# Values' products of the first four steps in other PSUM rings, sink rows on one queue, the next four steps' values two slots later

## The chip, the cores and the metric

The kernel runs on one core of a Trainium2 chip. The metric is the device time of one execution in microseconds (us). The engines are called PE (TensorE, matrix products), PEld (its weight loads), DVE (VectorE), ACT (ScalarE), POOL (GpSimd) and SP (SyncE, which issues most DMAs). Every engine works through its own list of instructions in order.

## The reference, cut to what matters

Attention with a sliding window of 128 keys and 4 sink keys over q, k, v of shape (4, 8, 768, 64), and then a feed-forward block over the 3072 rows of its result:

```python
keep = is_sink | in_window                 # rel in [0, 128) or key < 4
a = softmax(where(keep, scale * q @ k.T, -1e9))
x = (a @ v).transpose(0, 2, 1, 3).reshape(B * S, H * D)      # 3072 x 512
h = x @ w_in                               # 512 -> 2048
g = h * erf(softplus(h))
out = g @ w_out                            # 2048 -> 512
```

## The kernel before, in words

The 3072 rows are 12 groups of 256 tokens. Attention for a group is 4 steps, one per pair of heads, so step s belongs to group s // 4, and there are 48 steps. A step runs through these stages, each a small function in the code: `prep` transposes k and q on PE into a PSUM tile `tqk` and ACT copies it to `kq` (L299, L302, L305); `core` makes the scores `ps` on PE (L350), DVE adds the mask and takes the row maximum (L363, L368) and ACT the exponentials (L372); `norm` divides by the sums (L379 to L391, for steps 2 to 7 the division runs on ACT at L385); `ptrans` transposes the probabilities into PSUM tiles `tp` and `ts` (L403, L404), ACT copies them to `pa` and `pz` (L410 to L416) and POOL cuts the window's triangles out of them with four selects (L421); `av` multiplies them with the values on PE into a PSUM tile `av` (L452), from the values themselves and from `vz`, a tile that holds the sinks' 16 rows and half blocks of values; `xfin` copies the result to x on ACT (L465 for group 0; L470, and L471 on DVE, for the others).

PSUM has eight banks, dealt out as rings: `ps_o` two (tag o, the output sums), `ps_h` two (tag h, the hidden tiles), `ps_s` one tile of two banks (the scores), `ps_t` two (tag t: tqk, tp, ts and av take turns). A tile that takes a slot of a ring waits until the slot's last reader is done.

The feed-forward block goes by f: 16 blocks of 128 hidden units. A hidden tile h_m covers two f (L639 for group 0 in plain 32-bit products, L643 for the others in three products of split operands, called xh, xl and wt). ACT makes six activations of it (L656 to L661), DVE multiplies three of them together (L665, result gf, for the first two groups), and PE multiplies the result with w_out into the sums o (L685 for the first two groups, L688 to L690 for the others). The weights are 32 blocks (0 to 15 of w_in, 16 to 31 of w_out). They arrive as 64-bit floats (ws), and DVE turns each block into 32-bit with three passes (L541, L546, L549, result wf). All 32 are converted while groups 0 and 1 are under way.

The order of the work is set by a plan in slots (one slot per f): `plan[a]` lists what is emitted in slot a, `pos(s)` gives the slot of a step's scores (s for the first four steps, 3s - 6 for the next four), and a table of priorities goes with it. A scheduler then merges all engines' work by these priorities, so that a change of one slot or ring shuffles many neighbours. `norm` stands at pos + 1, `ptrans` at pos + 2, `av` at pos + 3, `xfin` at pos + 4. From step 8 on, av runs right before the scores of a later step.

In the first group the loads are issued in a list `head`. The sinks' rows for vz are eight small DMAs (`early_sinks(z, i, h)`): four for z = 1 on SP's queue, four for z = 0 on ACT's queue (L246), behind its first copy of keys (`mark["k"]`).

Of the kernel before, what the change touches and what calls it, by code (L numbers as in the profile page):

```python
# [9 lines left out]
F32 = mybir.dt.float32  # L10
# [9 lines left out]
P = 128  # L20
SW = 16
# [18 lines left out]
NE, AL = 4, 2  # L40
# [12 lines left out]
def kernel(  # L53
# [11 lines left out]
    nc = tc.nc  # L65
    B, H, S, D = q.shape
    NT, DM = out.shape
# [4 lines left out]
    GT = 256  # L72
# [58 lines left out]
    def fast_path():  # L131
        with ExitStack() as st:
# [5 lines left out]
            ps_o = st.enter_context(tc.tile_pool(name="ps_o", bufs=2, space=PSUM))  # L138
            ps_h = st.enter_context(tc.tile_pool(name="ps_h", bufs=2, space=PSUM))
            ps_s = st.enter_context(tc.tile_pool(name="ps_s", bufs=1, space=PSUM))  # L140
            ps_t = st.enter_context(tc.tile_pool(name="ps_t", bufs=2, space=PSUM))
# [25 lines left out]
            def set_rest():  # L167

                follow(mark["t", 0], nc.vector.tensor_tensor(mask[:, :P], kw[:, :128], kw[:, 128:256], op=ALU.max))
                set_mask(mask)  # L170
                set_flags(lambda ins: follow(mark["t", 0], ins))
# [10 lines left out]
            kq = pers.tile([P, NPAIR, 5, KB], F32, name="kq")  # L182
# [10 lines left out]
            mark = {}  # L193
# [49 lines left out]
            def early_sinks(z, i, h):  # L243

                r0 = HP * (1 - z) + 2 * SW * i + SW * h
                ins = (nc.sync if z else nc.scalar).dma_start(  # L246
                    vz[r0 : r0 + SW, z, i].rearrange("p (c h) d -> p c h d", h=2)[:, :, h],
                    v[0, :, :SW].rearrange("(c h) s d -> s c h d", h=2)[:, :, h],
                )
                if not z:  # L250
                    follow(mark["k"], ins)

            def early_dup(z, n):

# [3 lines left out]
            def next_dup():  # L258

                nc.sync.dma_start(vz[lo, 0], early[1, "v"][lo])  # L260
                for n in range(2):
                    nc.sync.dma_start(vz[hi, 1, n], early[n, "v"][hi, 1 - n])

            def dup(s):
# [3 lines left out]
                nc.sync.dma_start(vz[lo, 0, :, cs], t[lo, 1:])  # L268
                x = t[hi, 1:2].broadcast_to([HP, 2, 2, D]) if g % GPB == 0 else t[hi, :2]
                nc.sync.dma_start(vz[hi, 1, :, cs], x)  # L270

            def zero_sinks(s):

                for i in range(2):
                    for h in range(2):
                        early_sinks(0, i, h)

            def kcopy(s):

# [3 lines left out]
            def follow(prev, ins):  # L283

                if prev is not None:
                    tc.add_manual_dep(
                        ins.ins, prev.ins.name,
                        mybir.DependencyInfo(mybir.DependencyClass.NoSync, mybir.DependencyReason.DATA), reason="order",
                    )
                return ins  # L290

            def prep(s):

                g, c = divmod(s, NPAIR)
                d = stp[s]
                tp = ps_t.tile([P, 4, P], F32, tag="t", name=f"tqk_{s}")
                for j, t in enumerate((d["k"], d["q"])):
                    for i in range(2):
                        nc.tensor.transpose(  # L299
                            out=tp[:, 2 * j + i, :], in_=t[:, i].rearrange("p h d -> p (h d)"), identity=ident  # L300
                        )
                nc.scalar.copy(kq[:, c, 1:, :P], tp)  # L302
                if g % GPB == 0:
                    x = tp[:, 0, :SW].rearrange("p (o t) -> p o t", o=1)
                    mark.setdefault("k", nc.scalar.copy(kq[:, c, :3, P:], x.broadcast_to([P, 3, SW])))  # L305

            def core(s):

                prev = None
                late = s - AL >= 2 * NPAIR  # L310
                if late:
                    prev = av(s - AL)
                if s < NSTEP:
                    score(s, prev)
# [115 lines left out]
            def av(s):  # L430

                g, c = divmod(s, NPAIR)
                d = stp[s]
                gb = g % GPB
                a = d["av"] = ps_t.tile([P, GT], F32, tag="t", name=f"av_{s}")
                vt, pz = d["v"], d["pz"]
                pa = d["pa"].rearrange("p h i t -> p h (i t)")
                ops = []
                for j, (t0, t1) in enumerate(((0, HP), (HP, 3 * HP), (3 * HP, GT))):
                    if j > 0 or gb > 0:  # L440
                        x = vt[j] if isinstance(vt, list) else vt[:, j]
                        ops.append((x, pa[:, :, t0:t1], t0))
                for i in range(2):
                    for z, hf in enumerate((lo, hi)):
                        ops.append((vz[:, z, i, 2 * c : 2 * c + 2], pz[:, :, i, hf], P * i + HP * z))
                prev = mark.get(("p", s + 1)) if 0 < s < NE - 1 else None
                for m, (x, y, t0) in enumerate(ops):
                    for h in range(2):
                        o = a[64 * h : 64 * h + 64, t0 : t0 + y.shape[-1]]
                        prev = follow(  # L450
                            prev,
                            nc.tensor.matmul(  # L452
                                o, x[:, h, :], y[:, h, :], start=(m == 0), stop=(m == len(ops) - 1), skip_group_check=True
                            ),
                        )
                return prev
# [21 lines left out]
            def pos(s):  # L478

                return s if s < NE else 3 * s - 6 if s < 2 * NPAIR else 4 * s - 11  # L480

            plan = {}
            for s in range(NSTEP + AL):
                if s < NSTEP:
                    for what, fn, a in (
                        ("prep", prep, max(4, s - 1) if NE <= s < 2 * NPAIR else pos(s) - 3), ("norm", norm, pos(s) + 1), ("ptrans", ptrans, pos(s) + 2),
                        ("load", load, pos(s) - 4),
                    ):
                        if what == "load":
                            if s < 2 * NPAIR:  # L490
                                continue
                            plan.setdefault(a, []).append(("load", load_v, s))
                        plan.setdefault(max(a, 0 if what == "prep" else -1), []).append((what, fn, s))
                    if s >= 2 * NPAIR:
                        plan.setdefault(pos(s) - 2, []).append(("dup", dup, s))
                    if s // NPAIR % GPB < GPB - 1:
                        plan.setdefault(pos(s) + (2 if s < NE else 1), []).append(("kcopy", kcopy, s))
                plan.setdefault(pos(s), []).append(("core", core, s))
                if s < 2 * NPAIR:
                    plan.setdefault(pos(s) + 3, []).append(("av", av, s))  # L500
                    plan.setdefault(pos(s) + 4, []).append(("xfin", xfin, s))
                elif s - AL >= 2 * NPAIR:
                    plan.setdefault(pos(s) + 1, []).append(("xfin", xfin, s - AL))
            STAGES = ("xfin", "norm", "ptrans", "av", "kcopy", "prep", "core", "dup", "load")
# [66 lines left out]
            head = [(early_load, 0, "k", two[0]), (early_load, 0, "q", two[0], nc.scalar)]  # L571
            head += [(early_load, 0, nm, two[1]) for nm in "kq"] + [(wload, order[0])]
            head += [(early_load, 0, nm, four) for nm in "kq"] + [(early_load, 0, "v", slice(0, H))]
            head += [(early_dup, z, n) for z in range(2) for n in range(2)]
            head += [(early_sinks, 1, i, h) for i in range(2) for h in range(2)]
            head += [(wload, n) for n in order[1:4]]
            head += [(wload, order[4])] + [(early_load, 1, nm, slice(0, H)) for nm in "kq"]
            head += [(wload, n) for n in order[5:8]] + [(early_load, 1, "v", slice(0, H))] + [(wload, n) for n in order[8:W0]]
            for x, (fn, *args) in enumerate(head):
                with at(-1 + 4 * x / PW, "load"):  # L580
                    fn(*args)
            plan.setdefault(2 * NE, []).append(("dup", lambda s: next_dup(), NE))
            plan.setdefault(0, []).append(("load", zero_sinks, 0))
            plan.setdefault(2, []).append(("prep", lambda s: set_rest(), NSTEP))
            for m in range(-LEAD, NG * NF + LAG + 2):
                a = m + LEAD
                live = 0 <= m < NG * NF
                if live:
                    g, f = divmod(m, NF)
# [107 lines left out]
    def general_path():  # L697

        NT_S = S // P
        with ExitStack() as st:  # L700
# [71 lines left out]
            with tc.tile_pool(name="g_one1", bufs=1) as one, tc.tile_pool(name="g_work1", bufs=2) as work:  # L772
# [3 lines left out]
                with tc.For_i(0, B, 1) as b:  # L776
                    for gb in range(GPB):
# [25 lines left out]
                        for i in range(2):  # L803
# [3 lines left out]
                            )  # L807

    fast_path()
    ok = nc.values_load(flagi[0:1, 0:1], min_val=0, max_val=1)  # L810
    with tc.If(ok == 0):  # L811
# [31 lines left out]
```

## Time and profile before

| | |
|---|---|
| three runs, us | 748.79, 748.98 (median), 750.62 |
| the profiled execution: its time / its span, us | 748.7 / 746.5 |
| busy share PE, DVE, ACT, POOL | 96%, 65%, 74%, 28% |
| chain that ended last | PE, in the output products of the last group |

The shares are averages over the whole span; the change touches only the first 100 us, and from there on the instruction lists of both kernels soon run alike.

### The profile page before, as it was taken

To read this page: it belongs to the slowest core of one execution; us is meant where nothing else is said; L and a number is where in the kernel's file an instruction comes from. 1 tells how busy PE (TensorE), PEld (TensorE's weight loads), DVE (VectorE), ACT (ScalarE), POOL (GpSimd) and SP (SyncE) were. 2 spreads that over 40 slices of the span, in tenths; PEclk is the share of its full clock that TensorE was granted. 3 is DMA by queue.
4 is the path that set the end of the run, shared out by engine and by line. 5 is a ranking of instruction groups with operands and counts; after the bars stand their busy time and mean duration, and the time that the engine had idled before them with its cause. 6 is when DMAs were issued, how large, how long until landed. Compare 5 with 4: busy or idle time off the path is not lost. (4 is left out here: it accounts for less than half of the span.)

```text
span 746.5 us, 16409 instructions
## 1 busy us (share of the span) xinstructions
PE 717.5 (96%) x5808; PEld 598.3 (80%) x5808; DVE 487.1 (65%) x1367; ACT 553.7 (74%) x1317; POOL 207.0 (28%) x296
## 2 busy tenths in 40 slices
PE   5769999999899999999999999999999999999997
PEld 3557666766788888888888888888888898889885
DVE  6999976755676666665665665666566576475252
ACT  4687666984996975985985976886886786777572
POOL 1322412012242232233233234224223223333221
PEclk9689999999999999999999999999999999999999
DMA  7999311111312211311311321221221222200000
GB/s 148 301 318 363 88 29 43 35 34 43 87 34 57 79 37 43 83 37 42 79 41 46 80 47 34 74 50 40 69 54 41 76 48 45 61 18 2 29 1 33
DMA packets 115113, 53.60 MB, mean 72 GB/s; under 512 B 93840, under 2 KB 107664, under 8 KB 115024
## 3 DMA queue, kind: packets, MB, share of 16 engines
q1 hardware_dynamic: 114144, 52.33, 26.5%
q8 instruction: 49, 0.80, 0.4%
q14 instruction: 40, 0.33, 0.2%
q10 hardware_dynamic: 880, 0.13, 0.1%
HBM read 38.54 MB, written 6.29 MB: 60 GB/s over the span
## 5 line engine op out<-in xcount | busy, mean ns | idle before, releaser
L643 PE MATMUL h<-xh,wt 128*128 128x256 f32 x1408 | 277.8, 286 | 0.7 <-DVE u L665 0.7
L643 PEld LDWEIGHTS h<-xh,wt 128*128 128x128 f32 x1408 | 224.2, 188 | 7.5 <-DVE u L665 1.7
L673 POOL TENSOR_TENSOR g<-u,g 128x512 fp32r<-128x512 f32 x80 | 106.0, 1325 | 341.0 <-DVE g L672 337.3
L643 PE MATMUL h<-xl,wt 128*128 128x256 f32 x704 | 197.6, 281 | 0.0
L661 ACT ACTIVATE u<-r 128x512 f32<-128x512 f32 x288 | 161.8, 622 | 9.0 <-DMA out_dram<-ot 2.2
L643 PEld LDWEIGHTS h<-xl,wt 128*128 128x128 f32 x704 | 132.3, 188 | 4.5 <-issue 0.7
L665 DVE SCALAR_TENSOR_TENSOR u<-u,u 128x512 f32<-128x512 f32 x160 | 125.3, 783 | 15.2 <-ACT u L661 0.6
L689 PE MATMUL o<-wt,g 128*128 128x512 f32 x320 | 127.6, 399 | 0.0
L688 PE MATMUL o<-wt,g 128*128 128x512 f32 x320 | 127.5, 398 | 0.0
L690 PE MATMUL o<-wt,g 128*128 128x512 f32 x320 | 123.7, 398 | 0.2 <-POOLq L811 0.2
L665 DVE SCALAR_TENSOR_TENSOR u<-u,h 128x512 f32<-128x512 f32 x80 | 54.9, 686 | 85.1 <-ACT u L661 82.7
L421 POOL TENSOR_SCALAR_AFFINE_SELECT pz<-pa 64x256 f32<-64x256 f32 (+1 forms) x96 | 54.7, 569 | 171.1 <-ACT pa L410 167.9
L372 ACT ACTIVATE pst<-pst,neg 128x144 f32<-128x144 f32 x192 | 77.5, 406 | 23.3 <-DVE neg L368 22.4
L656 ACT ACTIVATE r<-h 128x512 f32<-128x512 f32 x96 | 56.5, 589 | 25.7 <-PE h L643 15.0
L688 PEld LDWEIGHTS o<-wt,g 128*128 128x128 f32 x320 | 60.1, 188 | 11.4 <-ACT ot L694 0.4
L690 PEld LDWEIGHTS o<-wt,g 128*128 128x128 f32 x320 | 59.1, 188 | 12.4 <-POOLq L811 0.7
L689 PEld LDWEIGHTS o<-wt,g 128*128 128x128 f32 x320 | 60.1, 188 | 10.5
L672 DVE CAST g<-u 128x512 fp32r<-128x512 f32 x80 | 34.9, 437 | 47.1 <-PE o L690 44.2
L657 ACT ACTIVATE r<-r 128x512 f32<-128x512 f32 x96 | 60.7, 632 | 2.5
L658 ACT ACTIVATE r<-r 128x512 f32<-128x512 f32 x96 | 60.6, 631 | 2.5
L685 PE MATMUL o<-wf,gf 128*128 128x512 f32 x128 | 57.8, 594 | 0.0
L410 ACT COPY pa<-tp 128x512 f32<-128x512 f32 x48 | 28.2, 587 | 30.5 <-PE tp L403 30.4
(86 smaller groups left out, 940.9 us busy)
## 6 DMA issues: line engine op xcount, KB each, us to landing
ws<-in_moe_w_in_dram SPq DMA_DIRECT2D x16, 512.0 KB, 5.9
ws<-in_moe_w_out_dram SPq DMA_DIRECT2D x16, 512.0 KB, 8.0
out_dram<-ot SPq DMA_DIRECT2D x24, 256.0 KB, 2.1
v<-in_v_dram SPq DMA_DIRECT2D x56, 96.0 KB, 2.3
q<-in_q_dram SPq DMA_DIRECT2D x80, 64.0 KB, 2.1
k<-in_k_dram SPq DMA_DIRECT2D x80, 64.0 KB, 2.1
vz<-v SPq DMA_DIRECT2D x80, 64.0 KB, 2.1
kq<-kq SPq DMA_DIRECT2D x28, 64.0 KB, 2.0
```

Source lines behind the costliest of these rows:

```text
L372: nc.scalar.activation(y, y, AF.Exp, bias=d["neg"][:, i, h : h + 1], scale=-1.0, accum_out=d["sum"][:, i, h : h + 1])
L643: last = nc.tensor.matmul(o, wt[NC * j + c][:, p, fs], xt[e][:, c, :], start=(m == 0), stop=(m == len(ops) - 1))
L656: nc.scalar.activation(r, h, AF.Tanh, bias=b_t, scale=0.5)
L657: nc.scalar.activation(r, r, AF.Square, bias=b_v, scale=-0.5)
L658: nc.scalar.activation(r, r, AF.Square, bias=b_r)
L661: sq = nc.scalar.activation(u, r, AF.Square, bias=b_a[i], scale=CS)
L665: pr = nc.vector.scalar_tensor_tensor(out=acc, in0=u, scalar=CC[i] * CS**2, in1=x, op0=ALU.add, op1=ALU.mult)
L673: nc.gpsimd.tensor_tensor(gl, acc, gh.bitcast(F32), op=ALU.subtract)
L685: nc.tensor.matmul(o, gt[0][:, ws], wf[16 + f], start=(f == 0), stop=(f == NF - 1))
L688: behind(nc.tensor.matmul(o, gh[:, ws], wt[16 + f][:, 0, :], start=(f == 0), stop=False))
L689: nc.tensor.matmul(o, gh[:, ws], wt[16 + f][:, 1, :], start=False, stop=False)
L690: nc.tensor.matmul(o, gl[:, ws], wt[16 + f][:, 0, :], start=False, stop=(f == NF - 1))
```

## The change

Three edits. The tile of av takes a slot of the hidden ring for steps 0 and 1, of the output ring for steps 2 and 3, and of ps_t as before from step 4 on. The four sink DMAs for z = 0 go on SP's queue, ahead of the four for z = 1, and no longer follow ACT's copy. For steps 4 to 7 av stands at pos + 5 and xfin at pos + 6.

```diff
             def early_sinks(z, i, h):
 
                 r0 = HP * (1 - z) + 2 * SW * i + SW * h
-                ins = (nc.sync if z else nc.scalar).dma_start(
+                nc.sync.dma_start(
                     vz[r0 : r0 + SW, z, i].rearrange("p (c h) d -> p c h d", h=2)[:, :, h],
                     v[0, :, :SW].rearrange("(c h) s d -> s c h d", h=2)[:, :, h],
                 )
-                if not z:
-                    follow(mark["k"], ins)
...
-                a = d["av"] = ps_t.tile([P, GT], F32, tag="t", name=f"av_{s}")
+                if s < 2:
+                    a = ps_h.tile([P, 2, GT], F32, tag="h", name=f"av_{s}")[:, 0, :]
+                elif s < NE:
+                    a = ps_o.tile([P, DM], F32, tag="o", name=f"av_{s}")[:, :GT]
+                else:
+                    a = ps_t.tile([P, GT], F32, tag="t", name=f"av_{s}")
+                d["av"] = a
...
                 if s < 2 * NPAIR:
-                    plan.setdefault(pos(s) + 3, []).append(("av", av, s))
-                    plan.setdefault(pos(s) + 4, []).append(("xfin", xfin, s))
+                    x = pos(s) + (3 if s < NE else 5)
+                    plan.setdefault(x, []).append(("av", av, s))
+                    plan.setdefault(x + 1, []).append(("xfin", xfin, s))
...
-            head += [(early_sinks, 1, i, h) for i in range(2) for h in range(2)]
+            head += [(early_sinks, z, i, h) for z in range(2) for i in range(2) for h in range(2)]
...
-            plan.setdefault(0, []).append(("load", zero_sinks, 0))
```

What the scheduler makes of it, at three places. In the names the first number is the step (for h, wf, ws, gf the block or the hidden unit's f), the last one a buffer. First PE's list around the values' product of step 0, in the kernel before:

```order
L403 MATMUL tp_1_346<-ident_61,pst_132 128x128 x4
L404 MATMUL ts_1_347<-ident_61,snk_1_276 128x128
L452 MATMUL av_0_364<-pa_0_285,v_early0_149 64x128 x2
L452 MATMUL av_0_364<-pa_0_285,v_early0_149 64x64 x2
L452 MATMUL av_0_364<-pz_0_286,vz_129 64x64 x8
L403 MATMUL tp_2_420<-ident_61,pst_132 128x128 x4
L404 MATMUL ts_2_421<-ident_61,snk_2_344 128x128
```

and in the changed kernel:

```order
L395 MATMUL tp_1_346<-ident_61,pst_132 128x128 x4
L450 MATMUL av_0_364<-pa_0_285,v_early0_149 64x128 x2
L450 MATMUL av_0_364<-pa_0_285,v_early0_149 64x64 x2
L396 MATMUL ts_1_347<-ident_61,snk_1_276 128x128
L450 MATMUL av_0_364<-pz_0_286,vz_129 64x64 x8
L395 MATMUL tp_2_420<-ident_61,pst_132 128x128 x4
L396 MATMUL ts_2_421<-ident_61,snk_2_344 128x128
L450 MATMUL av_1_438<-pa_1_353,v_early0_149 64x128 x2
L450 MATMUL av_1_438<-pa_1_353,v_early0_149 64x64 x2
```

The product of step 0 has moved ahead of the second transpose of step 1 (ts_1), and that of step 1 right behind step 2's transposes; before, step 1's product stood behind the first hidden products.

Second, PE's list around the transposes of step 4, where the product of step 4 stood. Before:

```order
L403 MATMUL tp_4_592<-ident_61,pst_132 128x128 x3
L404 MATMUL ts_4_593<-ident_61,snk_4_578 128x128
L403 MATMUL tp_4_592<-ident_61,pst_132 128x128
L350 MATMUL ps_6_765<-kq_128 64x208 x2
L350 MATMUL ps_6_765<-kq_128 64x224 x2
L350 MATMUL ps_6_765<-kq_128 64x208 x2
L350 MATMUL ps_6_765<-kq_128 64x224 x2
L452 MATMUL av_4_622<-pa_4_599,v_early0_149 64x64 x2
L452 MATMUL av_4_622<-pa_4_599,v_early1_180 64x128 x2
L452 MATMUL av_4_622<-pa_4_599,v_early1_180 64x64 x2
L403 MATMUL tp_5_702<-ident_61,pst_132 128x128
L639 MATMUL h_4_835<-xf_0_410,wf_4_469 128x256 x2
```

and in the changed kernel:

```order
L395 MATMUL tp_4_592<-ident_61,pst_132 128x128
L396 MATMUL ts_4_593<-ident_61,snk_4_578 128x128
L395 MATMUL tp_4_592<-ident_61,pst_132 128x128 x3
L637 MATMUL h_4_818<-xf_0_410,wf_4_469 128x256 x2
L637 MATMUL h_4_818<-xf_0_410,wf_6_560 128x256 x2
L637 MATMUL h_4_818<-xf_0_410,wf_4_469 128x256 x2
L637 MATMUL h_4_818<-xf_0_410,wf_6_560 128x256 x2
L342 MATMUL ps_6_750<-kq_128 64x208 x2
L342 MATMUL ps_6_750<-kq_128 64x224 x2
L342 MATMUL ps_6_750<-kq_128 64x208 x2
L342 MATMUL ps_6_750<-kq_128 64x224 x2
L683 MATMUL o_0_0_854<-wf_16_581,gf_1_715 128x512
```

Between the scores of step 6 and the hidden tile of f = 4 no product av_4 is left; it stands 24 rows further on, behind two groups of output products and the hidden tiles of f = 6 and f = 8. The scores of step 6 stand behind the hidden tile now, and those of step 5 right ahead of the transposes.

Third, DVE's list up to the last of the three products for the hidden tile of f = 8 (gf_9). Before:

```order
L665 SCALAR_TENSOR_TENSOR gf_9_1053<-u0_9_1057,h_8_1007 128x512
L546 SCALAR_TENSOR_TENSOR wf_24_923<-ws_24_691,wf_24_923 128x512
L546 SCALAR_TENSOR_TENSOR wf_24_923<-ws_25_696,wf_24_923 128x512
L665 SCALAR_TENSOR_TENSOR gf_9_1053<-u1_9_1060,gf_9_1053 128x512
L549 SCALAR_TENSOR_TENSOR wf_24_923<-ws_24_691,wf_24_923 128x512
L541 TENSOR_SCALAR wf_26_948<-ws_26_736 128x512
L549 SCALAR_TENSOR_TENSOR wf_24_923<-ws_25_696,wf_24_923 128x512
L541 TENSOR_SCALAR wf_26_948<-ws_27_741 128x512
L665 SCALAR_TENSOR_TENSOR gf_9_1053<-u2_9_1063,gf_9_1053 128x512
```

and in the changed kernel:

```order
L663 SCALAR_TENSOR_TENSOR gf_9_1036<-u0_9_1040,h_8_1005 128x512
L548 SCALAR_TENSOR_TENSOR wf_14_858<-ws_15_652,wf_14_858 128x512
L540 TENSOR_SCALAR wf_24_908<-ws_25_677 128x512
L545 SCALAR_TENSOR_TENSOR wf_24_908<-ws_24_672,wf_24_908 128x512
L383 TENSOR_TENSOR snk_7_926<-pst_132,sum_7_871 128x128
L663 SCALAR_TENSOR_TENSOR gf_9_1036<-u1_9_1043,gf_9_1036 128x512
L545 SCALAR_TENSOR_TENSOR wf_24_908<-ws_25_677,wf_24_908 128x512
L469 TENSOR_TENSOR xl_1_745<-av_5_839,xh_1_744 128x256
L548 SCALAR_TENSOR_TENSOR wf_24_908<-ws_24_672,wf_24_908 128x512
L540 TENSOR_SCALAR wf_26_931<-ws_26_732 128x512
L663 SCALAR_TENSOR_TENSOR gf_9_1036<-u2_9_1046,gf_9_1036 128x512
```

The last product (from u2_9) has one pass of the conversions less right ahead of it: the pass that ends block 25 (L549 before, L548 in the change) now follows it, and so does the first pass of block 27. In all, from the last row maximum of step 4 to this product, the changed list holds 54 conversion passes and 14 products gf, the list before 57 and 14.

## Rows read from the trace of the kernel before

**Rows 1.** Busy time by stretch: PE, PEld, DVE, ACT, POOL; granted clock, DMA share, GB/s.

```profile
17.00:31.00 14.00, 9.12 (x80) 6.77 (x77) 12.78 (x49) 10.74 (x40) 4.58 (x14) 0.52 0.94 259
31.00:51.00 20.00, 14.50 (x150) 11.33 (x148) 18.93 (x53) 14.23 (x41) 4.40 (x8) 1.00 1.02 327
51.00:58.00 7.00, 5.92 (x24) 4.79 (x25) 6.91 (x21) 5.69 (x17) 1.44 (x2) 0.52 1.01 279
58.00:94.00 36.00, 36.00 (x209) 24.00 (x207) 35.88 (x79) 26.19 (x59) 13.56 (x10) 1.00 0.65 221
...
103.00:746.00 643.00, 634.94 (x5230) 540.64 (x5229) 392.77 (x1096) 485.45 (x1127) 179.15 (x252) 1.00 0.19 48
```

**Rows 2.** List of waits on PE, first 110 us: total, times, longest.

```profile
PE av L452 <- POOL pa L421: 6.8, 4, 4.6
```

**Rows 3.** Timeline of PE, 18 to 31 us: start, duration, instruction, [idle before].

```profile
24.40 0.91 PE L452 MATMUL av<-pa,v_early 128*64 128x128 f32 x8 [4.88 <-ACT pz L416]
...
26.10 1.12 PE L403 MATMUL tp<-ident,pst 128*128 128x128 f32 x4
```

**Rows 4.** Timeline of ACT, 19 to 25 us.

```profile
22.26 1.28 ACT L385 ACTIVATE pst<-pst,sum 128x128 f32<-128x128 f32 x4 [0.98 <-DVE sum L380]
```

**Rows 5.** Timeline of PE, 44 to 62 us.

```profile
51.30 0.48 PE L452 MATMUL av<-pa,v_early 128*64 128x64 f32 x4 [4.61 <-POOL pa L421]
...
53.67 5.65 PE L639 MATMUL h<-xf,wf 128*128 128x256 f32 x16
...
59.58 0.99 PE L350 MATMUL ps<-kq 64*64 64x208 f32 x16
60.49 1.99 PE L685 MATMUL o<-wf,gf 128*128 128x512 f32 x4
```

**Rows 6.** Timeline of POOL, 44 to 97 us.

```profile
49.93 2.58 POOL L421 TENSOR_SCALAR_AFFINE_SELECT pa<-pa 64x256 f32<-64x256 f32 x2
...
86.85 8.08 POOL L421 TENSOR_SCALAR_AFFINE_SELECT pz<-pa 64x256 f32<-64x256 f32 x2 [6.01 <-ACT pa L410]
```

**Rows 7.** Timeline of PE, 44 to 170 us.

```profile
84.09 0.67 PE L452 MATMUL av<-pa,v_early 128*64 128x64 f32 x12
...
85.16 0.66 PE L403 MATMUL tp<-ident,pst 128*128 128x128 f32 x4
85.65 3.62 PE L639 MATMUL h<-xf,wf 128*128 128x256 f32 x16
89.11 3.60 PE L685 MATMUL o<-wf,gf 128*128 128x512 f32 x8
92.54 0.27 PE L404 MATMUL ts<-ident,snk 128*128 128x128 f32 x1
...
103.06 0.47 PE L643 MATMUL h<-xh,wt 128*128 128x256 f32 x1
```

**Rows 8.** Timeline of DVE, 36.5 to 40 and 85 to 88 us.

```profile
36.98 0.44 DVE L363 COPY_PREDICATED ps<-tri,ps 64x256 f32<-64x256 int8 x1
...
38.17 0.31 DVE L368 CUSTOM_DVE_ANT_0 pst<-ps,mask 128x144 f32<-128x144 f32 x1
...
39.09 0.69 DVE L549 SCALAR_TENSOR_TENSOR wf<-ws,wf 128x512 int32<-128x512 int32 x1
39.70 0.46 DVE L541 TENSOR_SCALAR wf<-ws 128x512 int32<-128x512 int32 x1
...
86.53 0.43 DVE L541 TENSOR_SCALAR wf<-ws 128x512 int32<-128x512 int32 x1
86.86 0.69 DVE L665 SCALAR_TENSOR_TENSOR gf<-u,gf 128x512 f32<-128x512 f32 x1
```

**Rows 9.** Timeline of SP's queue, 3 to 22 us.

```profile
9.86 0.92 SPq L241 DMA_DIRECT2D q_early<-in_q_dram  x2
...
15.60 2.14 SPq L246 DMA_DIRECT2D vz<-in_v_dram  x4
```

**Rows 10.** List of waits of SP's queue, first 60 us.

```profile
SPq L241 <- DMA vz<-in_v_dram: 3.3, 1, 3.3
```

More of the change, by code (lines that the diff above doesn't have):

```diff
@@ L270, in dup @@
                 nc.sync.dma_start(vz[hi, 1, :, cs], x)
[L272 to L276, printed above, removed]
             def kcopy(s):
@@ L304, in prep @@
                     x = tp[:, 0, :SW].rearrange("p (o t) -> p o t", o=1)
-                    mark.setdefault("k", nc.scalar.copy(kq[:, c, :3, P:], x.broadcast_to([P, 3, SW])))
+                    nc.scalar.copy(kq[:, c, :3, P:], x.broadcast_to([P, 3, SW]))
             def core(s):
```

## The prediction

> **What bounds the kernel now.** I read the stretches first: busy time by engine, in windows. Behind 103 us PE is busy 634.94 of 643 us at full clock, and the changed list soon runs like the old one there: a tail that only moves. In the head the engines take turns. From 31 to 94 us DVE is almost never idle (18.93 of 20, 6.91 of 7, 35.88 of 36 us): it converts the weights. PE is idle 5.5 us of the stretch from 31 to 51 and, at a granted clock of about half (0.52: mostly the lower level of 1.2 GHz), again in that from 51 to 58; from 58 to 94 it is busy throughout [rows 1]. Then the list of waits on PE: over the first 110 us the longest item is that for POOL's selects, 6.8 us in four pieces, all in front of values' products [rows 2].
>
> Then the places. PE's largest wait is 4.88 us ahead of the values' product of step 0 at 24.40 us [rows 3]. The trace puts it down to ACT's copy of pz (L416). That copy is of step 1: step 0's product takes the ring slot that step 1's transposes held. The wait isn't POOL's, so its own operands were cut before that. The next large one stands ahead of step 4's product: 4.61 us until 51.30, for step 4's selects. What follows it, the hidden tile of f = 4, takes 5.65 us where a tile of as many records takes 3.62 at full clock [rows 5, 7]. The reader is to see that PE's list is in order: an unfinished product holds up hidden tiles whose weights have long been ready.
>
> **The change part by part.**
>
> *Other rings for steps 0 to 3.* No instruction is added; tiles of one bank stay tiles of one bank. The wait of 4.88 us ahead of step 0's product loses its reason. What stands behind it gains less: step 2's transposes need ACT's normalization of step 2, four instructions from 22.26 for 1.28 us, so about 23.5 [rows 4]. They start at 26.10 before; at most 2.6 us of the 4.88 can be passed on. DVE's list up to step 4 stays in nearly the same order, and DVE had hardly a gap, so little of this reaches it. I mark DVE's place by the last row maximum of step 4, which ends at 39.1 us [rows 8], and take its gain as nothing, with bounds of 1 us earlier and 1 us later: later, if PE's idle time at 20 us, now spread differently, keeps the lower clock longer than 31 us. The hidden tiles of f = 0 and 2 now follow these products in the hidden ring; they need their x anyway, so that costs nothing.
>
> *Sinks' rows on SP.* Four DMAs leave ACT's queue and join SP's. The four that were there take 2.14 us to issue from 15.60 [rows 9], so four more delay all weight loads behind them by 2.1 us. But SP also loses a wait: it stood 3.3 us before issuing q at 9.86, for the transfers of ACT's four [rows 9, 10]. Net, the loads go out about 1.2 us earlier; if that wait stays in another form they are 2.1 us later. Even then the last of eight is issued at about 20 us, before step 0's product ran in the old kernel. I cost this part at nothing, cover: DVE, busy with earlier blocks.
>
> *Values of steps 4 to 7 two slots later.* The 4.61 us, and with them most of the 6.8 us of waits for POOL, go, because two output groups and two hidden tiles now stand between step 4's transposes and its product. That is PE's side. PE can't take all of this forward, since the work pulled ahead needs DVE's conversions and products gf. So I compute both sides to one place, the first three-way hidden product of group 1, at 103.06 us before [rows 7].
>
> DVE's side. The gate is the third product gf for the hidden tile of f = 8, which starts at 86.86 us and takes 0.69 us [rows 8]. From the mark at 39.1 to there the changed list has 54 conversion passes in place of 57 and otherwise the same kinds and numbers. A long pass costs 0.61 us (39.09 to 39.70), a first pass 0.33 (86.53 to 86.86) [rows 8]; two long ones and a first one less make 1.55 us. So the product ends at 87.55 - 1.55 = 86.0 us. Behind it PE's new list has one output group (89.11 to 92.54, 3.43 us), step 6's product (84.09 to 85.16, 1.07), two pairs of transposes (as the four at 85.16 to 85.65, 0.49), a hidden tile (85.65 to 89.11, 3.46) and three products of the next output group (3/4 of 3.43, 2.57) [rows 7]: 11.0 us, to 97.0.
>
> PE's side. It starts with the third product of the first hidden pair. Ahead of that, behind the mark, DVE's new list holds 11 long passes (6.71), 6 first ones (1.98), four row maxima (0.92, 38.17 to 39.09), two mask copies (0.44 each) [rows 8], and three small ones that I put at 0.4: an end at 39.1 + 10.9 + 0.7 = 50.7. From there PE has four output groups (13.7), four hidden tiles (13.8), two values' products (2.1), three steps' transposes (0.5 each, some 0.3 for the sinks') and one set of scores (0.91, 59.58 to 60.49) [rows 5, 7]: 32.3 us, to 83.0, 3.0 us before DVE's 86.0. So DVE sets the place, and 3 us are left for a stretch at the lower clock (2.0 us per hidden tile, 5.65 less 3.62).
>
> The sum: 103.06 - 97.0 = 6.0 us. At this place PE has three output products more behind it (2.57) and step 7's values' product (1.07) fewer: 1.5 us more work done. Together 7.5 us. Afterwards DVE has room, and the tail is PE's. The profiled execution took 748.7 us, 2.2 outside its span of 746.5, and lies 0.3 under the median of 748.98. So 746.5 - 7.5 is a span of 739.0, 741.2 with what lies around it, and against the median 741.5 us. The unknown mark (1 us either way) and 1 us either way for the short waits that move give 739.5 to 743.5 for this case.
>
> **A rule against the change.** Two selects of step 7 took 8.08 us from 86.85, while two of step 4 took 2.58 and DVE was full in both places [rows 6]. The changed list leaves all selects of steps 4 to 7 in that stretch. The Trainium skill (SBUF — State Buffer, section "SBUF: two separate sides") says that VectorE instructions with two SBUF inputs and GpSimd share a pair of ports, an exclusive lock in which the loser waits a whole instruction. The 8.08 us agree with that; by the rule the later products could wait as before and the last term would fall away, by the sum they don't.
>
> **The rivals.** First, PE's side decides: idle spells around 42 to 50 us (PE must wait there for the first products gf) bring the lower clock for more than one stretch of 7 us. At 2.0 us per tile of 3.5 us, two such stretches cost about 7, 3 of them covered: gain 3.5, 745.5 us. For it speaks the clock of 0.52 behind the wait until 51.30 [rows 1]; against it, that this happened once in the head after 31 us.
>
> Second, no change: DVE's in-order list meets products gf earlier than ACT has their operands. The first one moves up by five microseconds, and each microsecond that it waits is lost at 86.0. If the first hidden tile isn't finished earlier than before, that is 5 to 7 us: 747 to 749 us. Against it: with the values' products ahead of them gone, the first tiles should be done some us sooner.
>
> Third, slower: step 7's selects. Its product stands about 1.5 us behind the place at 97.0. Two pairs at 8.08 us behind copies at some 84 us would end at 100.5 and cost 2 us. It decides against the change only if a pair takes over 12 us, ending past 108: then the whole 7.5 us are gone and 2.3 more, 751.3 us. No pair in the trace is longer than 8.08.
>
> Fourth, a gain of more than 9.5 us: the mark over 1 us earlier and DVE's small gaps closed, 738.5 us.
>
> **How the numbers follow.** Chances: the forecast 0.52, the lower clock 0.22, no change 0.13, slower 0.06, more gain 0.07. About 0.3% (2.2 us) is what a measurement of this kernel can tell from no change: faster (under 746.7) 0.81, same 0.13, slower 0.06. The range leaves out most of the no-change case, the slower one and a little of the largest gain: 738.5 to 747.4.
>
> **What would show it.** Right: no wait of PE for POOL around 50 us and none of 4.9 us ahead of step 0's product; the hidden tile of f = 4 done near 50 us, ten earlier; a wait of PE for DVE's gf near 83 to 86; the first three-way product of group 1 near 97; the tail's length the same. Wrong: DVE idle for microseconds between 40 and 60 (second rival), granted clock under 1 over more than 7 us behind 31 (first), a values' product behind 97 us that waits for POOL (third), or loads later than their conversions (the SP part).

## The result, and the profile after

The changed kernel takes 741.02 us (median of four runs, 740.61 to 741.60) against 748.88 us (four runs, 748.70 to 750.62): a ratio of 0.989 with a 95% interval of 0.9873 to 0.9908, 7.9 us faster. The profiled execution took 741.2 us with a span of 739.1, 7.4 us less than the 746.5 of before.

First the stretches again, as in [rows 1]: PE, PEld, DVE, ACT, POOL; granted clock, DMA share, GB/s.

```profile
17.00:31.00 14.00, 8.71 (x75) 6.29 (x75) 12.56 (x47) 10.94 (x40) 5.68 (x14) 0.88 0.95 271
31.00:51.00 20.00, 17.02 (x136) 13.11 (x137) 18.73 (x47) 14.74 (x37) 4.51 (x8) 0.91 0.96 299
51.00:58.00 7.00, 6.94 (x37) 4.03 (x36) 6.91 (x18) 4.87 (x14) 0.00 (x0) 1.00 1.03 299
58.00:94.00 36.00, 35.64 (x218) 23.40 (x217) 35.84 (x84) 27.09 (x67) 9.26 (x12) 1.00 0.66 226
...
103.00:739.00 636.00, 627.88 (x5191) 536.34 (x5189) 391.50 (x1097) 478.88 (x1118) 176.39 (x252) 1.00 0.20 48
```

From 31 to 58 us PE is busy 23.96 of 27 us, before 20.42 [rows 1]. DVE is as full as it was. The granted clock from 17 to 31 us rose from 0.52 to 0.88, while from 31 to 51 us it fell from 1.00 to 0.91; DVE shows no gain from the rise: its last row maximum of step 4 comes 0.8 us later than before. The tail kept its idle time: 636 less 627.88 is 8.1 us, as 643 less 634.94 was.

The list of waits on PE in the first 110 us (total, times, longest), which answers to [rows 2]:

```profile
PE tp L395 <- ACT pz L408: 4.5, 2, 3.6
PE h L637 <- DVE gf L663: 2.6, 1, 2.6
PE ps L342 <- ACT pst L364: 1.2, 1, 1.2
PE tp L395 <- ACT pst L377: 0.8, 2, 0.4
...
PE av L450 <- POOL pa L413: 0.2, 1, 0.2
```

The 6.8 us for POOL have become 0.2. The places themselves, in the timeline of PE, for [rows 3, 5, 7]:

```profile
18.39 0.71 PE L450 MATMUL av<-pa,v_early 128*64 128x128 f32 x8 [0.21 <-POOL pa L413]
...
23.58 1.11 PE L395 MATMUL tp<-ident,pst 128*128 128x128 f32 x4 [3.61 <-ACT pz L408]
...
46.31 5.38 PE L637 MATMUL h<-xf,wf 128*128 128x256 f32 x16 [2.57 <-DVE gf L663]
51.62 0.99 PE L342 MATMUL ps<-kq 64*64 64x208 f32 x16
52.67 3.70 PE L683 MATMUL o<-wf,gf 128*128 128x512 f32 x8
...
81.86 0.33 PE L395 MATMUL tp<-ident,pst 128*128 128x128 f32 x1 [0.36 <-ACT pst L377]
...
86.86 3.66 PE L683 MATMUL o<-wf,gf 128*128 128x512 f32 x8
...
97.64 0.68 PE L641 MATMUL h<-xh,wt 128*128 128x256 f32 x1
...
99.58 0.67 PE L450 MATMUL av<-pa,v_early 128*64 128x64 f32 x12
...
109.87 0.99 PE L342 MATMUL ps<-kq 64*64 64x208 f32 x16 [1.24 <-ACT pst L364]
```

Step 0's product starts at 18.39 in place of 24.40, and step 2's transposes at 23.58. The hidden tile of f = 4 (46.31) waits for the first product gf and still takes 5.38 us. The output products begin at 52.67, before at 60.49. From there to 109.87 PE's only wait is the 0.36 us at 81.86, for step 7's normalization. The first three-way product stands at 97.64, and step 7's product at 99.58 waits for nobody.

DVE's timeline, for [rows 8]: the last row maximum of step 4, the third gf of the first hidden tile, the reciprocal of step 7, the third gf for f = 8.

```profile
39.67 0.30 DVE L360 CUSTOM_DVE_ANT_0 pst<-ps,mask 128x144 f32<-128x144 f32 x1
...
51.93 0.69 DVE L663 SCALAR_TENSOR_TENSOR gf<-u,gf 128x512 f32<-128x512 f32 x1
...
81.19 0.18 DVE L372 RECIPROCAL sum<-sum 128x4 f32<-128x4 f32 x1
...
86.07 0.69 DVE L663 SCALAR_TENSOR_TENSOR gf<-u,gf 128x512 f32<-128x512 f32 x1
```

### The profile page after: what moved, and what is told of

Same layout as the page of the kernel before. It is cut to its first block, busy times and chain, and to the rows that moved or that the text cites. A ratio compares the mean times of both kernels' runs of the same rounds, so it can differ in the third digit from the quotient of the medians.

```text
span 739.1 us, 16411 instructions
## 1 busy us (share of the span) xinstructions
PE 715.4 (97%) x5808; PEld 595.0 (81%) x5808; DVE 486.0 (66%) x1367; ACT 552.5 (75%) x1317; POOL 197.6 (27%) x296
## 5 line engine op out<-in xcount | busy, mean ns | idle before, releaser
L413 POOL TENSOR_SCALAR_AFFINE_SELECT pz<-pa 64x256 f32<-64x256 f32 (+1 forms) x96 | 47.6, 496 | 173.2 <-ACT pa L402 169.8
L294 ACT COPY kq<-tqk 128x512 f32<-128x512 f32 x48 | 27.9, 583 | 35.2 <-PE tqk L291 34.1
```

## The experiments

Every time is a median and stands with the ratio to the kernel before and its interval. The first four runs were made beside a median of 748.83 us for the kernel before, the next four beside 749.02, the last four beside 748.14.

**The edits one by one.** The third edit alone, the first alone, the second alone, and the change without its second edit:

```diff
-                    plan.setdefault(pos(s) + 3, []).append(("av", av, s))
-                    plan.setdefault(pos(s) + 4, []).append(("xfin", xfin, s))
+                    x = pos(s) + (3 if s < NE else 5)
+                    plan.setdefault(x, []).append(("av", av, s))
+                    plan.setdefault(x + 1, []).append(("xfin", xfin, s))
```

> The kernel before with the third edit alone (values of steps 4 to 7 at pos + 5); rings and sinks as before. Theory S (the slots carry the gain, the two other edits are worth nothing): 741 to 742.5 us, no wait of PE for POOL near 50 us, the wait of about 4.9 us ahead of step 0's product still there. Rival R (the rings' 4.88 us are a part of the gain): 743.5 us or more, since only the part of the slots is left.

Measured: 743.19 us, 0.9933 (0.9913 to 0.9953): between the two theories, most of the gain but not all of it. The wait for POOL near 50 us is gone; the one ahead of step 0's product is still there (5.50 us).

```diff
-                a = d["av"] = ps_t.tile([P, GT], F32, tag="t", name=f"av_{s}")
+                if s < 2:
+                    a = ps_h.tile([P, 2, GT], F32, tag="h", name=f"av_{s}")[:, 0, :]
+                elif s < NE:
+                    a = ps_o.tile([P, DM], F32, tag="o", name=f"av_{s}")[:, :GT]
```

> The kernel before with the first edit alone (rings of the values' products of steps 0 to 3). Theory S: 748 to 749.5 us, the 4.88 us ahead of step 0's product go and most of them come back ahead of step 2's transposes; the wait for POOL near 51 us stays. Rival R: up to 2.6 us of the 4.88 are passed on, 746.3 to 747 us.

Measured: 747.42 us, 0.9993 (0.9977 to 1.0009): no difference. As theory S has it, 2.93 us come back ahead of step 2's transposes, and the wait for POOL stays (4.89 us, until 53.11).

```diff
-                ins = (nc.sync if z else nc.scalar).dma_start(
+                nc.sync.dma_start(
...
-                if not z:
-                    follow(mark["k"], ins)
```

> The kernel before with the second edit alone (all eight sink rows on SP's queue). Theory S: 748 to 749.5 us. Rival L (loads later by up to 2.1 us, conversions with them): 750 to 751 us, with DVE waiting for ws. Rival E (SP's wait of 3.3 us gone, loads 1.2 us earlier and DVE with them): 747.7 us.

Measured: 750.27 us, 1.0022 (1.0010 to 1.0034): slightly slower, but not by theory L. DVE waits 0.2 us for loaded blocks there. PE waits 5.64 us for step 7's selects, of which two took 12.23 us. The timelines of PE and POOL in that run:

```profile
100.18 1.39 PE L444 MATMUL av<-pa,v_early 128*64 128x64 f32 x12 [5.64 <-POOL pa L413]
```

```profile
87.41 12.23 POOL L413 TENSOR_SCALAR_AFFINE_SELECT pz<-pa 64x256 f32<-64x256 f32 x2 [10.08 <-ACT pa L402]
```

This is the mechanism of the third rival, in a list in which step 7's product stands earlier.

> The change without its second edit: rings and later slots, sink rows on two queues as before. In the changed kernel the last row maximum of step 4 ends at 39.99 us, 0.8 later than in the kernel before, and DVE waits 0.9 us for loaded blocks in place of 0.3. If the sinks on SP did that (theory L'), it goes here: mark near 39.2, first three-way product near 96.8, 740.2 us. If the rings did it or it is of no weight (S): 741 us as the change, within 0.3.

Measured: 744.72 us, 0.9954 (0.9935 to 0.9972). Both expectations missed: without the second edit the change loses almost 4 us of its gain and is slower than the slots alone (743.19). In the timeline of PE in this run:

```profile
46.04 0.99 PE L350 MATMUL ps<-kq 64*64 64x208 f32 x16
51.15 1.35 PE L403 MATMUL tp<-ident,pst 128*128 128x128 f32 x4 [4.12 <-ACT pst L385]
52.37 5.60 PE L646 MATMUL h<-xf,wf 128*128 128x256 f32 x16
```

The wait for POOL is gone, but one of 4.12 us has taken its place at the same time: the transposes of step 5 stand ahead of the hidden tile of f = 4 in this list and wait for step 5's normalization. With the slots alone a wait of the same kind is 4.85 us, until 52.76. In the changed kernel the scores of step 5 stand behind the hidden tiles of f = 0 and 2, and step 5's transposes come only at 63 us. So the second edit seemed to act through the order that the scheduler makes.

**Is it the order or the queue?** The change without its rings; the changed kernel with only the place of step 5's scores turned back; the changed kernel with four sink DMAs on ACT's queue; and the changed kernel again beside them.

> The change without its first edit: sinks on SP and later slots, the values' products of steps 0 to 3 in the old ring. In this list the hidden tiles of f = 0 and 2 stand ahead of the scores of step 5, as in the changed kernel. Theory O (the order on PE around step 5's scores and the transposes of step 5 decides, and the sinks' edit is what turned it round): 740.5 to 742 us, like the change; the rings are worth nothing. Rival R (rings and slots together): 743.5 us or more, as with the slots alone (743.2) or without the sinks (744.7).

Measured: 741.29 us, 0.9894 (0.9877 to 0.9912). The rings are worth nothing; sinks and slots together are the change.

```diff
+                mark["ps", s] = prev
...
-                    nc.tensor.matmul(o, wf[NC * j + c][:, fs], xt[0][:, c, :], start=(c == 0), stop=(c == NC - 1))
+                    x = nc.tensor.matmul(o, wf[NC * j + c][:, fs], xt[0][:, c, :], start=(c == 0), stop=(c == NC - 1))
+                    if f < 4 and c == NC - 1:
+                        self.behind5(x)
...
+            mlp.behind5 = lambda ins: follow(mark["ps", 5], ins)
```

> The changed kernel with one place of PE's list turned back: the scores of step 5 stand ahead of the last products of the hidden tiles of f = 0 and 2 again, as in the run without the sinks' edit. DVE then meets the row maxima of step 5 ahead of the first product gf. Theory O1 (the place of these scores carries the sinks' share): 743.5 to 745 us, first product gf near 50 us in place of 45.5. Theory O2 (the transposes of step 5 ahead of the hidden tile of f = 4 carry it; here they stay behind it): 740.5 to 742 us.

Measured: 742.88 us, 0.9917 (0.9902 to 0.9932). It lies between O1 and O2. The first product gf came at 49.88, as O1 said, and all five executions (742.36 to 743.73) lie above the four of the changed kernel beside them (740.75 to 742.06). So the place of these scores seems to carry about 1.3 us, a part of the sinks' share; the intervals against the kernel before overlap, so this stays weak.

```diff
-                nc.sync.dma_start(
+                (nc.sync if z else nc.scalar).dma_start(
```

> The changed kernel with the four sink DMAs for z = 0 issued from ACT's queue, in the changed place of the code (no longer behind the first copy of keys). The hidden tiles stay ahead of step 5's scores, and all three products of the first pair of f stand ahead of step 5's row maxima on DVE. Theory O (order decides, not the queue): 739.5 to 741.5 us. Rival Q (the queue itself carries it: SP's wait of 3.3 us behind ACT's four DMAs comes back and loads come later): 743.5 us or more.

Measured: 742.80 us, 0.9920 (0.9905 to 0.9934). By neither: this list is another one again, with a wait of 2.8 us for step 2's normalization, and SP's wait of 3.3 us didn't come back.

> The changed kernel once more, on the chip of the other runs of this set, as their base: 740.5 to 742 us by every theory.

Measured: 741.58 us, 0.9903 (0.9886 to 0.9920).

As long as each edit makes a new list, no run separates queue and order. So in the last set the lists of PE, DVE, ACT and POOL are held, instruction by instruction, to those of the changed kernel, by order constraints alone (their numbers are left out; a helper records the instructions, so all lines of these kernels read L75):

```diff
+            for e, runs in LISTS.items():
+                seq = [log[e][i0 + i] for i0, n in runs for i in range(n)]
+                for one, two in zip(seq, seq[1:]):
+                    tc.add_manual_dep(
+                        two, one.name,
+                        mybir.DependencyInfo(mybir.DependencyClass.NoSync, mybir.DependencyReason.DATA), reason="order",
+                    )
```

> The kernel of the run with rings and later slots and the sink rows on two queues as before (744.72 us there), but with its lists of PE, DVE, ACT and POOL held to those of the changed kernel. What is left of the second edit is then the queue alone. Theory O (the sinks' edit is worth 3.7 us through the lists): 740.7 to 742.3 us. Rival Q (the queue itself, four DMAs on ACT and SP's wait behind them): 744 us or more.

Measured: 741.88 us, 0.9918 (0.9900 to 0.9936), by theory O. The same four DMAs stand on ACT's queue as in the run of 744.72, and SP's wait of 3.3 us for their transfers is back. Yet all six executions (740.56 to 742.86) lie below those of that run (744.30 to 745.51), and the time is that of the change within the intervals. By the ratios the lists give back 0.0036, some 2.7 us; the other 1 us or so lies within the intervals and could be the queue's. So the second edit works in the main through the lists.

**What sets the gate?** With held lists, work can be cut without moving anything. In the first of three runs the long conversion passes of blocks 14 and 15 work on 32 of 512 columns (later passes), in the second those of blocks 18 and 19 (earlier passes), and in the third PE makes half of some products:

```diff
+                e = 32 if n in (14, 15) else DM
...
-                    out=ti, in0=w[:, :, 0], scalar=29, in1=ti, op0=ALU.logical_shift_right, op1=ALU.bitwise_or
+                    out=ti[:, :e], in0=w[:, :e, 0], scalar=29, in1=ti[:, :e], op0=ALU.logical_shift_right, op1=ALU.bitwise_or
```

> The changed kernel with its lists of PE, DVE, ACT and POOL held as they are, and the four long conversion passes of blocks 14 and 15 (at 78.98 to 82.55 us in the changed kernel's trace, between the first products gf and the third one for f = 8) cut to 32 of 512 columns; the rest of these two blocks' weights is left half converted. That takes some 2.0 us from DVE ahead of the gate. Theory D (the prediction's: DVE alone sets the gate, PE reaches it 3 us earlier): about 2 us faster than the changed kernel, 739 us. Theory B (PE and DVE reach it together, since PE's work from the first output product at 52.67 us is without a gap until 86.86): no change, 740.7 to 741.8 us, and PE no later or earlier at the first three-way product (97.6).

Measured: 738.96 us, 0.9883 (0.9865 to 0.9900): theory D's time. The changed kernel wasn't run with held lists and its whole work; against the nearest runs beside this one, 741.01 (half products, below) and 741.88 (held lists, above), it is 2 to 3 us faster, and no execution overlaps theirs. Two rows of PE's timeline in it:

```profile
80.63 0.27 PE L75 MATMUL tp<-ident,pst 128*128 128x128 f32 x1
...
107.13 0.99 PE L75 MATMUL ps<-kq 64*64 64x208 f32 x16
```

These are the transposes of step 7 and the scores at 109.87 above, both without their waits now. In this execution PE was 0.71 us ahead already at the first output product (51.96), which the cut can't have caused; behind the transposes it is 1.42 us ahead, behind these scores 2.74, and the span is 736.5, 2.6 less. So 2.0 us come from the two places where PE waited for ACT, whose operands DVE makes. At the gate itself the third gf for f = 8 ended at 84.03, 2.7 us earlier, but PE reached the output products behind it at 85.50, only 1.36 us earlier: there DVE no longer set the place.

> The same, lists held, but the four long passes of blocks 18 and 19 cut (43.5 to 50.0 us, ahead of the third product gf of the first hidden pair, with which PE's run begins). Again some 2.0 us less on DVE, now ahead of both sides. Theory B: PE's run begins 1.5 to 2 us earlier and DVE's gate is as much earlier, 739 to 739.8 us. Theory D: 739 us too. Rival C (the time is set by neither, what is gained at 52 us is lost to other waits or to the lower clock): 740.7 us or more.

Measured: 738.53 us, 0.9878 (0.9860 to 0.9896), as B and D said; the first output product is 1.04 us earlier, the rest came at the same two places.

```diff
+                    e = P if 6 <= f < 12 and c in (1, 2) else GT
-                    nc.tensor.matmul(o, wf[NC * j + c][:, fs], xt[0][:, c, :], start=(c == 0), stop=(c == NC - 1))
+                    nc.tensor.matmul(
+                        o[:, :e], wf[NC * j + c][:, fs], xt[0][:, c, :e], start=(c == 0), stop=(c == NC - 1)
+                    )
```

> The changed kernel with its lists held, and 12 of the 24 products of the hidden tiles of f = 6 to 11 over 128 in place of 256 tokens (the other half of these terms is left out). That takes 12 halves of 0.43 us, 2.2 to 2.6 us, from PE between 56 and 74 us. Theory P (PE alone sets the gate): 738.5 us. Theories B and D (DVE's third product gf for f = 8 can't be earlier): PE waits for it at 84 to 86.8 us, no change, 740.7 to 741.8 us.

Measured: 741.01 us, 0.9907 (0.9890 to 0.9924): nothing, as B and D said. But PE didn't wait at the gate that they name. Its timeline:

```profile
69.51 1.21 PE L75 MATMUL tp<-ident,pst 128*128 128x128 f32 x4 [0.88 <-ACT pst L75]
...
82.46 0.33 PE L75 MATMUL tp<-ident,pst 128*128 128x128 f32 x1 [1.30 <-ACT pst L75]
```

About 2.5 us of products less became, for the most part, waits for the normalizations of steps 6 and 7. So PE does have slack against DVE, but it runs out in front of transposes, not of products gf.

## Why the prediction was right, step by step

- **The time and the sum.** 741.5 us forecast, 741.02 measured; the likeliest case came. Term by term: the third gf for f = 8 ended at 86.76 (86.0 forecast), PE took 10.78 us from 86.86 to 97.64 (11.0 forecast, to 97.0), and from there to the span's end there are 641.46 us against 643.44, 1.98 less (1.5 forecast). The gate came 0.8 us late, the two terms behind it were 0.2 and 0.5 us better than forecast, and the errors nearly cancel: that the span came out at 739.1 for 739.0 is in part luck.
- **Three conversion passes less.** From the conversion pass behind the last row maximum of step 4 to the start of that gf it took 46.17 us (39.90 to 86.07), before 47.77 (39.09 to 86.86, [rows 8]): 1.60 us less, 1.55 forecast. But only 1.0 us of that is the passes': counted from start to start, the 54 passes took 30.05 us, the 57 before 31.06. The rest came from idle time and the short instructions of the normalizations, which the forecast held equal, so this agreement too is in part luck. The mark came 0.8 us later, inside its bounds. In this trace DVE waits 0.9 us for loaded blocks, but with the sinks on two queues and the same lists it waited 0.3 and the mark stood at 40.4, so the loads alone are not the reason, and the cause stays open.
- **Rings worth nothing.** Right. Step 2's transposes stand at 23.58, forecast 23.5, and the change without the rings is as fast (0.9894 and 0.9903).
- **Sinks' rows on SP "at nothing".** This step was wrong, though the sum wasn't. As a queue it is worth little or nothing (held lists, 741.88): SP's wait of 3.3 us went, but the weight loads behind the sinks' rows went out only 0.7 us earlier than with two queues and the same lists (17.11 and 17.80; 1.2 forecast). But it belongs to the list from which the sum was worked out: without it the change stops at 744.72. The sum was right because it was read from the whole new list; its division among the edits was not.
- **DVE sets the place, PE has 3 us left.** Right in direction: cutting DVE by four passes gave about 2 us, cutting PE by 2.5 us nothing. Wrong in place and in PE's term: PE came to the gate at 86.86, 0.1 us behind DVE, and the forecast wait for gf at 83 to 86 us didn't come. The 3 us had gone into a later start (52.67, forecast 50.7) and into 34.2 us of work in place of 32.3, of which 0.36 is a wait. PE is held 5 us earlier, at step 7's transposes, and again at 109.87, each time by ACT, which starts on what DVE has just finished (at 81.41 on the reciprocal of 81.19, at 109.11 on a row maximum).
- **The rivals.** The lower clock (first) came, in one stretch behind the wait of 2.57 us: 5.38 us for a tile of 3.62. It was covered, though not by the 3 us: the output products behind it needed the third gf, which ended at 52.62. In the second profile of the changed kernel the same tile took 6.58 us, and that execution took 740.75 us. The second, DVE waiting for ACT's operands, didn't come: DVE's list of waits has none in front of a product gf. The third, step 7's selects: the pair took 2.42 us here and no product waited for it, but in the run with the sinks alone it took 12.23 us and PE waited 5.64 us.
- **The hidden tile of f = 4** was done at 51.69, 7.6 us earlier, not ten.

## What to carry to other kernels

Where a scheduler merges the lists, price the whole new list and not the edits: an edit that costs little or nothing in itself (four DMAs on another queue) was worth some 3 to 4 us, for the most part through what it moved, and one that takes away PE's largest single wait (the rings, 4.88 us) was worth nothing that shows. To find out which engine sets a stretch, hold the lists and cut work on one engine at a time; a row without a wait in front of it doesn't show that the engine has no slack. When a wait is removed, look for the next operand of the same in-order engine: with the slots alone, 4.61 us for POOL became 4.85 us for ACT at the same place.

## What the runs showed of the hardware

A select on POOL takes 0.3 to 3.1 us in most places, but seven of them, in six of the kernels, took 5.30 to 9.10 us (the 8.08 us of [rows 6] hold one of 7.03). Two of them, in the timeline of all engines, first with the slots alone, then in the changed kernel with four sink DMAs on ACT's queue:

```profile
79.73 8.23 POOL L421 TENSOR_SCALAR_AFFINE_SELECT pz<-pa 64x256 f32<-64x256 f32 x1
87.00 0.67 DVE L547 SCALAR_TENSOR_TENSOR wf<-ws,wf 128x512 int32<-128x512 int32 x1
...
87.61 0.41 DVE L471 TENSOR_TENSOR xl<-av,xh 128x256 fp32r<-128x256 f32 x1
```

```profile
90.91 8.83 POOL L413 TENSOR_SCALAR_AFFINE_SELECT pz<-pa 64x256 f32<-64x256 f32 x1
...
98.79 0.67 DVE L558 TENSOR_TENSOR wt<-wf,wt 128x512 fp32r<-128x512 f32 x1
...
99.39 0.67 DVE L663 SCALAR_TENSOR_TENSOR gf<-u,h 128x512 f32<-128x512 f32 x1
```

The first ends at 87.96, 0.35 us after DVE started an instruction that reads av in PSUM; the second at 99.74, 0.35 us after one that reads h in PSUM. Six of the seven end 0.35 to 0.37 us after such a start; the seventh (9.10 us, sinks alone) ends 0.28 us after DVE fell idle. Before that, 10 to 16 instructions ran on DVE beside each of these selects, back to back, all with SBUF operands alone. So these seven lasted until DVE's next instruction with an operand in PSUM, or its next gap. In the changed kernel such an instruction stands at 88.21, 1.6 us behind the start of step 7's selects; in the kernel before it came at 94.56, and the 8.08 us of [rows 6] ended at 94.93.

It is not a rule for every select. Behind step 7's first pair the changed kernel has these two:

```profile
89.12 1.57 POOL L413 TENSOR_SCALAR_AFFINE_SELECT pa<-pa 64x256 f32<-64x256 f32 x2
```

They took 0.75 us each, though DVE ran without a gap and its next instruction with an operand in PSUM started only at 94.23; beside them DVE's passes took up to 0.89 us in place of 0.69. Over all traces, 46 selects between 40 and 110 us had neither such an instruction nor a gap of DVE in the 2.5 us behind their start, and 36 of them were done within 1.2 us. What lets one select through and holds another stays open.

The Trainium skill (SBUF — State Buffer, section "SBUF: two separate sides") says that VectorE instructions in a two-port mode or with two SBUF inputs and GpSimd instructions lock their shared ports against each other, and that the loser is blocked for the whole instruction of the other. The traces agree with a lock, but the prediction's reading that the 8.08 us agree with this rule goes too far: the seven selects lasted 10 to 16 instructions of DVE and not one. No run moved such an instruction on purpose, so this is read from the traces and not tried.
